# An MLP kernel in three stages: all up products, results kept in DRAM, then all down products as seven block products

## The chip, the cores and the metric

The kernel runs on one core of one Trainium2 chip. The metric is device time of one execution in microseconds (us), the median of several runs. TensorE is called PE, VectorE DVE, ScalarE ACT, GpSimd POOL; SP is the engine whose queue issues most loads.

## The reference

Four batches of 448 tokens. Attention with 12 heads of 64 and capped scores gives x (448 x 768 per batch); a low-rank product over the tokens (U, V, rank 32) is added to it; then comes a two-layer MLP of width 3,072 with a residual.

```python
def _attn_ref(q, k, v, cap):
    scores = scale * np.matmul(q, k.transpose(0, 1, 3, 2))
    scores = cap * np.tanh(scores / cap)
    ...
    attn = np.exp(scores)
    attn = attn / (np.sum(attn, axis=-1, keepdims=True) + 1e-09)
    return np.matmul(attn, v).astype(np.float32)

def _moe_ref(x, U, V, w_ch1, w_ch2):
    xt = x.transpose(0, 2, 1)
    h = xt @ U @ V
    u = x + h.transpose(0, 2, 1)
    ch = np.maximum(u @ w_ch1, 0.0) @ w_ch2
    return (u + ch).astype(np.float32)
```

All is float32. On PE a float32 product of the MLP is made of three matmuls on fp32r operands: each operand is split into a high and a low part (ACT copies the high part, DVE subtracts to get the low one), and high x high, high x low and low x high are added in PSUM.

## The kernel before

The program is written as a list of tasks, each with the engines that it can run on, an estimated duration, the buffers that it reads and writes, and a priority. A planner (`Plan.simulate`, lines 133 to 228) walks through time with these estimates, hands out buffers of the pools as they come free, and so fixes the order of instructions on every engine; `emit` then writes them in that order. Nothing is reordered on the chip: each engine executes its own list, and waits where an operand or a buffer is not ready.

The token activations after attention are u0 to u3, one for each batch, with the 768 features on partitions (six blocks of 128) and the 448 tokens in a row.

*Up products* (`up_seven`, matmuls on line 867). The batches go in two pairs, (0, 1) and (2, 3). The 24 blocks of 128 hidden features go in 12 chunks of two. For a pair and a chunk, the two halves of the 768 features, the two blocks and the two batches make a 2 x 2 by 2 x 2 block product, done by Strassen's scheme in seven products of nine matmuls (three feature blocks times the three parts), 63 matmuls of 128 x 128 by 448 for each chunk. Its operands are sums and differences: x for the activations (seven tiles for a pair, built once for each pair by `operands` and `part`, lines 695 and 702) and ws for the weights (built for each chunk from wa, `strassen_weights`). Results go from PSUM through cx, are added up (line 880), and pass a relu. The up products make 1,512 matmuls.

*Weights.* Both matrices arrive as 64-bit words; `convert` (lines 309, 314, 317) turns a raw block wr of 768 KB into 384 KB of float32 wa, which ACT's queue also stores to DRAM (kept, line 728) so that the second pair of batches loads it from there (line 718).

*Down products.* For the first pair (`down`, line 948) each chunk is followed by 12 plain products of six matmuls, interleaved with the up products of the next chunk by their priorities. For the second pair, the first ten chunks are joined in twos (QUADS = 5) and the down product of four hidden blocks is done in seven products (`down_seven`, line 1075; operands in `down_operands`, lines 994 and 1001), 126 matmuls for each; the last two chunks take the plain way. Together 1,008 plain matmuls and 630 in seven products. The results are added into u, either by DVE from PSUM (lines 953, 1093) or by a copy to st on ACT and an accumulating DMA on POOL's queue (lines 961, 1098), which the code calls a pour.

*Attention* (`four`, `normalize`, `mixin`) stands ahead of all this on PE and overlaps only a little with the first chunk. The sums over keys for the softmax are matmuls with a block of ones (line 585); for heads from number ALONE = 12 on, the part of the keys that is left over (64 of 448) has four small matmuls of its own for each pair of heads (line 588, in the profile each counted twice), while for the first 12 heads DVE adds it beforehand (line 552, 64 x 896).

## Time and profile before

| | |
|---|---|
| median of 3 runs | 842.54 us (842.36 to 843.48) |
| the profiled execution | 842.78 us, its span 841.0 us |
| PE busy | 832.0 us (99%) |
| DVE, ACT, POOL busy | 675.6, 498.2, 123.5 us |
| HBM read, written | 79.28 MB, 24.47 MB |

The profile is one execution. Busy times are from the first to the last of overlapping instructions; matmuls are pipelined, so their single durations (0.366 us) are longer than the distance between two of them. What ended an engine's idle time is inferred from semaphores.

### The profile page before, as it was taken

The page shows a single profiled execution, that of the slowest core. Times are in us where ns is not written, and L with a number is a line of the kernel's source. Part 1 is how long each engine was busy: PE and PEld are TensorE (multiplying, and loading weights), DVE is VectorE, ACT ScalarE, POOL GpSimd, SP SyncE. Part 2 cuts the span into 40 slices and gives each one's busy share as a digit, 9 for nine tenths or more (in the row PEclk, how much of TensorE's full clock was granted, in tenths as well). Part 3 has the DMA queues.
Part 4 walks back from the last instruction along what each step waited for, and adds up shares of the span by engine and source line. Part 5 has one row for each costly group of instructions (what it writes and reads, how often), then busy time and mean ns, then how long its engine had stood idle before and what let it go on. Part 6 is the DMA issues. An engine that isn't in the chain of part 4 may idle for free.

```text
span 841.0 us, 12164 instructions
## 1 busy us (share of the span) xinstructions
PE 832.0 (99%) x4524; PEld 663.2 (79%) x4524; DVE 675.6 (80%) x1141; ACT 498.2 (59%) x748; POOL 123.5 (15%) x162
## 2 busy tenths in 40 slices
PE   9999999999999999999999999999999999999998
PEld 4343333337899999999999999999999999999997
DVE  4778999659878878887888899698797887978764
ACT  7989999876545544454455445365565555555510
POOL 0111111111111111111111112001121111211200
PEclk9999999999999999999999999999999999999999
DMA  6456554513878867867686747526346263642413
GB/s 228 132 158 208 152 179 121 168 46 117 254 217 220 262 198 216 237 189 214 205 266 160 207 102 192 148 60 157 71 97 152 44 157 78 134 108 44 103 32 131
DMA packets 47612, 129.64 MB, mean 154 GB/s; under 512 B 6178, under 2 KB 23618, under 8 KB 47554
## 3 DMA queue, kind: packets, MB, share of 16 engines
q1 hardware_dynamic: 23024, 79.29, 29.7%
q0 software_dynamic: 17616, 30.71, 20.1%
q10 hardware_dynamic: 6914, 18.88, 5.7%
q8 instruction: 35, 0.57, 0.3%
q14 instruction: 23, 0.19, 0.1%
HBM read 79.28 MB, written 24.47 MB: 123 GB/s over the span
## 4 chain that ended last, share of the span: by engine, by line
PE 95%; DVE 2%; DMA 1%; ACT 1%; issue 1%; POOL 0%; DVEq 0%; POOLq 0%; ACTq 0%
PE mm L867 36%; PE mm L948 24%; PE mm L1075 15%; PE sc L488 8%; PE o L546 6%; PE misc L662 1%; PE o L531 1%; PE misc L585 1%; PE misc L405 1%; DMA rd<-r 1%; PE misc L651 1%; PE misc L635 1%; DVE x L702 1%; DMA rb<-rd 0%; PE misc L588 0%
## 5 line engine op out<-in xcount | busy, mean ns | idle before, releaser
L867 PE MATMUL mm<-x,ws 128*128 128x448 f32 x1512 | 330.7, 366 | 0.8 <-ACT cx L263 0.8
L867 PEld LDWEIGHTS mm<-x,ws 128*128 128x128 f32 x1512 | 283.3, 188 | 27.5 <-ACT cx L263 1.8
L948 PE MATMUL mm<-g,w 128*128 128x448 f32 x864 | 187.0, 366 | 0.0
L948 PEld LDWEIGHTS mm<-g,w 128*128 128x128 f32 x864 | 162.1, 188 | 13.8 <-issue 0.2
L1075 PE MATMUL mm<-g,w 128*128 128x448 f32 x630 | 139.2, 366 | 0.0
L1075 PEld LDWEIGHTS mm<-g,w 128*128 128x128 f32 x630 | 118.3, 188 | 9.7
L263 ACT ACTIVATE st<-mm 128x448 f32<-128x448 f32 x109 | 59.2, 543 | 80.7 <-PE mm L948 48.7
L961 POOL DMA_DIRECT2D u<-st x60 | 51.7, 862 | 272.3 <-ACT st L263 272.3
L953 DVE TENSOR_TENSOR u<-u,mm 128x448 f32<-128x448 f32 x108 | 66.1, 618 | 29.3 <-PE mm L948 28.9
L488 PE MATMUL sc<-qk 64*128 64x448 f32 (+1 forms) x384 | 77.4, 571 | 0.4 <-ACT th L495 0.4
L506 ACT ACTIVATE th<-th,capt 128x1792 f32<-128x1792 f32 x42 | 75.3, 1792 | 0.8
L495 ACT ACTIVATE th<-sc 128x896 f32<-128x896 f32 x80 | 69.6, 915 | 5.1 <-PE sc L488 4.9
L1098 POOL DMA_DIRECT2D u<-st x45 | 38.9, 864 | 211.6 <-ACT st L263 174.1
L488 PEld LDWEIGHTS sc<-qk 64*128 64x128 f32 (+1 forms) x384 | 27.6, 175 | 41.3 <-issue 18.1
L546 PE MATMUL o<-th,vn 128*64 128x448 f32 x280 | 57.9, 548 | 0.0
L263 ACT ACTIVATE cx<-mm 128x448 f32<-128x448 f32 x42 | 22.9, 546 | 57.4 <-PE mm L867 49.3
L702 DVE TENSOR_TENSOR ws<-ta,ws 128x384 fp32r<-128x384 f32 x96 | 52.8, 554 | 3.1 <-ACT ws L263 2.2
L263 ACT ACTIVATE ws<-ta 128x384 fp32r<-128x384 f32 x57 | 29.5, 520 | 34.6 <-PE mm L867 22.6
L317 DVE SCALAR_TENSOR_TENSOR wa<-wa,wr 128x768 int32<-128x768 int32 (+2 forms) x50 | 46.6, 932 | 4.0 <-ACT wa L309 3.3
L263 ACT ACTIVATE ws<-wa 128x384 fp32r<-128x384 f32 x51 | 26.0, 520 | 39.5 <-PE mm L867 39.5
L552 DVE TENSOR_TENSOR es<-es,th 128x896 f32<-128x896 f32 (+1 forms) x36 | 39.1, 1086 | 11.6 <-ACT th L506 10.9
L309 ACT ACTIVATE wa<-wr 128x768 f32<-128x768 f32 (+2 forms) x50 | 44.3, 888 | 6.9 <-DVE cx L880 1.9
(123 smaller groups left out, 932.3 us busy)
## 6 DMA issues: line engine op xcount, KB each, us to landing
wr<-in_w SPq DMA_DIRECT2D x48, 768.0 KB, 6.7
u<-st POOLq DMA_DIRECT2D x105, 224.0 KB, 4.2
kept<-wa ACTq DMA_DIRECT2D x48, 384.0 KB, 6.4
wa<-kept SPq DMA_DIRECT2D x28, 384.0 KB, 3.7
qk<-in_qk SPq DMA_DIRECT2D x23, 448.0 KB, 4.1
wr<-kept SPq DMA_DIRECT2D x20, 384.0 KB, 4.0
vn<-in_v SPq DMA_DIRECT2D x12, 448.0 KB, 3.9
rb<-rd POOLq DMA_DIRECT2D x24, 224.0 KB, 3.8
```

The costliest lines, as they stand in the source:

```text
L263: e.activation(out=out, in_=in_, func=func)
L317: nc.vector.scalar_tensor_tensor(out=a_t().bitcast(I32), in0=a_t().bitcast(I32), scalar=3, in1=raw_t()[:, 0::2], op0=ALU.logical_shift_lef ...
L488: nc.tensor.matmul(ps.t[out, a, :S], qks[c].t[hd, 1, 128 * t:min(S, 128 * t + 128)], qks[c].t[hd, 0], start=True, stop=True)
L495: nc.scalar.activation(out=th.t[:, j], in_=ps.t[:, :, :S], func=AF.Tanh, scale=(self.half if t == 3 else self.qsc) if raw else 1.0)
L506: nc.scalar.activation(out=th.t, in_=th.t, func=AF.Exp, scale=self.capt)
L546: nc.tensor.matmul(o.t[64 * a:64 * a + 64, :S], vn.t[:, 3 * i + t, a], th.t[:, j, a], start=False, stop=t == 2)
L702: e.tensor_tensor(out=lo, in0=src(), in1=hi.bitcast(F32), op=ALU.subtract)
L867: nc.tensor.matmul(ps.t[:, :S], ws[p].t[:, wi, sl], xs[p].t[:, xi, d], start=fresh and n == 0, stop=n == 8, skip_group_check=not fresh)
L948: nc.tensor.matmul(ps.t[:, :S], w1[f].t[:, wi, sl], g[b, f].t[:, gi], start=f == fs[0] and i == 0, stop=f == fs[-1] and i == 2)
L953: nc.vector.tensor_tensor(out=u.t[:, d], in0=u.t[:, d], in1=ps.t[:, :S], op=ALU.add)
L961: nc.gpsimd.dma_start(out=u.t[:, d], in_=st.t, accum_op=ALU.add)
L1075: nc.tensor.matmul(ps.t[:, :S], w[:, wi, k, sl], g[gi][:, k], start=fresh and n == 0, stop=n == 5, skip_group_check=not fresh)
```

## The change

The MLP runs in three stages. First come the up products of the pair (0, 1), then those of the pair (2, 3), both for all 12 chunks with no down products in between (`moe`, `up_seven`). Each result, 448 values on 128 partitions, is stored to DRAM (mid) by POOL's queue as soon as its relu is done. Then `down_all` makes all down products: the 24 hidden blocks form six quads m, two quads form a group, and for each group and each of the seven products the weights are built and split once and used for both pairs of batches (n); for each pair three output blocks of 12 matmuls are made. Two quads add up in one PSUM bank. That is 3 x 7 x 2 x 3 x 12 = 1,512 matmuls. `down`, `down_operands`, `down_seven`, `last_sums` and `weights` are removed.

The second weight matrix is converted block by block when there is room (SECONDS: 4 blocks in the first stage, 12 in the second, 8 in the first group of the third) and stored in DRAM by quads; stage 3 loads its weights (wb) and tokens (gq, gw) from DRAM. Every third result is poured (EVERY = 3), except in the last two products. For all heads DVE now adds the left-over keys (RESTS = 24). The pools are cut anew: attention has four more th tiles, stage 3 takes over memory of closed pools. The planner has a model of the transfer time of DMAs (size).

```diff
-QUADS = 5
-PORDER = 2, 3, 1, 6, 5, 7, 4
+GROUPS = (0, 1), (2, 3), (4, 5)
+EVERY = 3
+SECONDS = (0, 0, 1, 0, 1, 0, 1, 0, 1, 0, 0, 0), (0, 0, 1, 1, 1, 1, 1, 2, 1, 2, 1, 1), (2, 2, 2, 2)
+PORDER = 2, 1, 3, 6, 5, 7, 4
...
-FILL, FIRST = 14, 3
+RESTS = 24
+FILL, FIRST = 11, 3
...
+            done = now + cost + OVER.get(e, 0) + (LAT[e] if t.lat is None else t.lat)
+            if t.size:
+                self.moved = max(self.moved, now + cost + 1800) + t.size
+                done = max(done, self.moved + 500)
+            heapq.heappush(events, (done, 2, t.i, "d"))
...
-        self.wp = Pool("wp", {"wa": 2, "w1": 3, "g": 3, "ws": 4, "ta": 3}, shared={"gp": "g"})
+        self.wp = Pool("wp", {"wa": 2, "ws": 4, "ta": 3})
-        self.pre = Pool("pre", {"th": 3, "qk": 2, "es": 2})
-        self.xe = Pool("xe", {"x": 3, "cx": 2}, after=(self.pre,), shared={"st": "cx"})
+        self.pre = Pool("pre", {"th": 7, "qk": 2, "es": 2})
+        self.wg = Pool("wg", {"wl": 2, "wb": 2, "g": 3}, after=(self.pre,), shared={"wa": "wb"})
+        self.xe = Pool("xe", {"x": 3, "cx": 2}, after=(self.pre,), under=(self.wg,))
...
+        self.wc = Pool("wc", {"wb": 4}, after=(self.late,), within=(self.wp, "ws"))
+        self.wt = Pool("wt", {"wt": 2}, after=(self.late,), within=(self.wp, "wa"))
+        self.cl = Pool("cl", {"gq": 9, "st": 2}, after=(self.xe,))
+        self.cr = Pool("cr", {"wb": 4, "wt": 2, "wl": 1, "wr": 1, "wa": 1, "gq": 2, "g": 4}, after=(self.late,), side="right")
...
-                if p < ALONE:
+                if p < RESTS:
...
+            if which:
+                m, k, j = f // 4, f // 2 % 2, f % 2
+                if (m, j) not in self.quads:
+                    self.quads[m, j] = self.dp.tile([128, 2, DM], F32, tag="quad", name="quad", bufs=NF // 2)
+                nc.scalar.dma_start(out=self.quads[m, j][:, k], in_=a.t)
+                return
...
+            ws = None if n else self.strassen_weights(0, True, 60000, ALONE - 90)
...
+                prio = 3 if n or c < NCH - 2 else -60
+                ws = ws or self.strassen_weights(c, n == 0, 0, prio)
+                for _ in range(SECONDS[n][c]):
+                    self.block(1, next(seconds), True, 0, 3)
+                self.up_seven(n, c, xs, ws, order)
+                ws = None
+                order += 21
+        self.down_all(order, seconds)
...
+        if not begin:
+            at = iter([order - 4, *at][:1] + list(range(order + 3, order + 21, 3)))
...
+        def result(b, j, x):
+            self.task({"ACT": 560}, lambda: self.copy(nc.scalar, to(x), to(x), AF.Relu), r=[key(x)], w=[key(x)], prio=-200)
+            store(b, j, x)
+        def store(b, j, x):
+            at = n, c // 2, b, j
+            def out():
+                if at not in self.mid:
+                    self.mid[at] = self.dp.tile([128, 2, S], F32, tag="mid", name="mid", bufs=2 * NF)
+                nc.gpsimd.dma_start(out=self.mid[at][:, c % 2], in_=to(x))
+            self.task({"POOL": 1000}, out, r=[key(x)], w=[("mid", at, c % 2)], lat=4000, size=620, prio=-200)
...
+    def down_all(self, order, seconds):
...
+        for ms in GROUPS:
+            a, b, s2, w, g, bank = {}, {}, {}, {}, {}, {}
+            last = ms is GROUPS[-1]
+            for x, p in enumerate(PORDER):
+                for _ in range(SECONDS[2][x - 3] if ms is GROUPS[0] and x > 2 else 0):
+                    self.block(1, next(seconds), True, 0, prio, (self.cr,))
+                for m in ms:
+                    for i, j in {2: ((0, 1),), 1: ((0, 0),), 3: ((1, 0), (1, 1))}.get(p, ()):
...
+                for n in range(2):
+                    for m in ms:
+                        at = {2: (1, 0), 3: (1, 1), 1: (0, 0), 6: (0, 1), 7: (1, 0)}.get(p)
+                        if at:
+                            b[(m, n, *at)] = token(m, n, *at)
...
+                        if p == 6:
+                            term(b01, b11, ALU.subtract, b01, size)
+                            term(b00, b01, ALU.add, b00, size)
+                        if p == 5:
+                            term(b11, b11, ALU.subtract, b00, size)
+                        if p == 7:
+                            term(b10, b10, ALU.subtract, b00, size)
+                        src = {3: b11, 1: b00, 6: b00, 5: b11, 2: b10, 7: b01, 4: b10}[p]
+                        hi, lo = g[p, n, m] = [self.buf("g", [128, 2, S], F32R, self.wg, *self.gx, self.cr) for _ in range(2)]
+                        split(src, (hi, lambda hi=hi: hi.t), (lo, lambda lo=lo: lo.t), size)
+                for n, bs in enumerate(((0, 1), (2, 3))):
+                    u0, u1 = (self.u_bufs[i] for i in bs)
+                    for d in range(3):
+                        fresh = p not in (6, 5, 4)
+                        if fresh:
+                            bank[p == 3, n, d] = self.bank()
+                        ps = bank[p == 3, n, d]
+                        def products(p=p, n=n, d=d, ps=ps, fresh=fresh, w=w, g=g, ms=ms):
+                            sl = slice(128 * d, 128 * d + 128)
+                            at = [(m, k, wi, gi) for m in ms for k in range(2) for wi, gi in ((0, 0), (0, 1), (1, 0))]
+                            for i, (m, k, wi, gi) in enumerate(at):
+                                nc.tensor.matmul(
+                                    ps.t[:, :S], w[p, m].t[:, wi, k, sl], g[p, n, m][gi].t[:, k], start=fresh and i == 0,
+                                    stop=i == len(at) - 1, skip_group_check=not fresh)
+                        self.task({"PE": 6 * 206 * len(ms)}, products, r=[
...
+                        onto = {3: ((u1, d),), 1: ((u0, d),), 6: ((u0, 3 + d),), 5: ((u1, d), (u1, 3 + d)), 2: ((u0, d),),
+                            7: ((u1, 3 + d),), 4: ((u0, 3 + d),)}[p]
+                        for u, e in onto:
+                            count += 1
+                            self.onto(ps, lambda u=u, k=e: u.t[:, k], (u, e), count % EVERY == 0 and not (last and p in (7, 4)))
+                            if last and p in (1, 5, 7, 4) and (p != 5 or e < 3):
+                                self.task({"SP": 350}, lambda u=u, k=e, i=bs[u is u1]: nc.sync.dma_start(
+                                    out=self.out[i, 128 * k:128 * k + 128], in_=u.t[:, k]), r=[(u, e)], lat=2500, size=700, prio=-200)
```

On PE, in the steady part of the first pair, before (mm is the PSUM bank, x and ws the up operands, g the relu'd tokens, w1 the second weights):

```order
L948 MATMUL mm_2285<-g_2090,w1_1992 128x448 x3
L948 MATMUL mm_2285<-g_2139,w1_2222 128x448 x3
L948 MATMUL mm_2297<-g_2090,w1_1992 128x448 x3
L948 MATMUL mm_2297<-g_2139,w1_2222 128x448 x3
L867 MATMUL mm_2306<-x_1125,ws_2150 128x448 x9
L948 MATMUL mm_2323<-g_2090,w1_1992 128x448 x3
L948 MATMUL mm_2323<-g_2139,w1_2222 128x448 x3
L948 MATMUL mm_2333<-g_2090,w1_1992 128x448 x3
L948 MATMUL mm_2333<-g_2139,w1_2222 128x448 x3
L867 MATMUL mm_2272<-x_1056,ws_2176 128x448 x9
```

and on PE in the changed kernel, its whole list from the last steps of attention (misc) to the end:

```order
L812 MATMUL mm<-x,ws 128x448 x9
L672 MATMUL misc<-vst,ys 128x448 x2
L812 MATMUL mm<-x,ws 128x448 x27
L645 MATMUL misc<-ident,u_1401 112x64 x16
L812 MATMUL mm<-x,ws 128x448 x9
L661 MATMUL misc<-xx,ust 32x128 x8
L812 MATMUL mm<-x,ws 128x448 x9
L672 MATMUL misc<-vst,ys 128x448 x2
L812 MATMUL mm<-x,ws 128x448 x1413
L958 MATMUL mm<-g,wl 128x448 x12
L812 MATMUL mm<-x,ws 128x448 x9
L958 MATMUL mm<-g,wl 128x448 x1500
```

Up and down products no longer alternate; one set of 12 down matmuls stands ahead of the last nine up matmuls.

On DVE, where the x operands of the second pair are built (u_1002, u_1451 are u2 and u3; wr holds the differences), before:

```order
L265 CAST x<-wr 128x448 x2
L702 TENSOR_TENSOR x<-wr,x 128x448 x3
L953 TENSOR_TENSOR u_562<-u_562,mm 128x448
L695 TENSOR_TENSOR wr<-u_1002,wr 128x448 x3
L880 TENSOR_TENSOR cx<-cx,mm 128x448
L702 TENSOR_TENSOR x<-wr,x 128x448 x2
L835 SCALAR_TENSOR_TENSOR g<-cx,g 128x448
L953 TENSOR_TENSOR u_562<-u_562,mm 128x448
L702 TENSOR_TENSOR x<-wr,x 128x448
L695 TENSOR_TENSOR wr<-u_1002,u_1451 128x448
```

and in the changed kernel (u_974, u_1401 are u2 and u3):

```order
L274 CAST x<-wr 128x448 x2
L712 TENSOR_TENSOR x<-wr,x 128x448 x3
L705 TENSOR_TENSOR wr<-u_974,wr 128x448
L825 TENSOR_TENSOR cx<-cx,mm 128x448
L705 TENSOR_TENSOR wr<-u_974,wr 128x448
L712 TENSOR_TENSOR x<-wr,x 128x448
L705 TENSOR_TENSOR wr<-u_974,wr 128x448
L712 TENSOR_TENSOR x<-wr,x 128x448
L825 TENSOR_TENSOR cx<-cx,mm 128x448
L712 TENSOR_TENSOR x<-wr,x 128x448
L705 TENSOR_TENSOR wr<-u_974,u_1401 128x448 x3
L712 TENSOR_TENSOR x<-wr,x 128x448 x3
```

The adds of down products (line 953) and the low parts of g (line 835) are gone from between, and the operands of different products follow each other directly.

On SP's queue, before, in the part of the second pair with seven products (wa and wr are loads of kept weights):

```order
L718 DMA wa<-kept 128x768 x5
L982 DMA wr<-kept 128x768 x2
L718 DMA wa<-kept 128x768
L982 DMA wr<-kept 128x768 x2
L718 DMA wa<-kept 128x768 x4
L982 DMA wr<-kept 128x768 x4
```

and in the changed kernel from the first loads of stage 3 on (wb weights, gq and gw tokens, wr raw blocks of the second matrix):

```order
L884 DMA wb<-quad 128x2x384 x2
L891 DMA gq<-mid 128x896 x2
L891 DMA gw<-mid 128x896
L884 DMA wb<-quad 128x2x384 x4
L891 DMA gw<-mid 128x896
L734 DMA wr<-in_w 128x1536
L884 DMA wb<-quad 128x2x384 x2
L891 DMA gq<-mid 128x896 x9
L884 DMA wb<-quad 128x2x384 x2
L734 DMA wr<-in_w 128x1536 x2
```

Tokens, which stayed in SBUF before, are now loads on this queue, 448 KB each, beside the weights.

## Rows read from the trace of the kernel before

**Rows 1.** The page: busy times, granted clock in tenths, chain by engine.

```profile
PE 832.0 (99%) x4524; PEld 663.2 (79%) x4524; DVE 675.6 (80%) x1141; ACT 498.2 (59%) x748; POOL 123.5 (15%) x162
...
PEclk9999999999999999999999999999999999999999
...
PE 95%; DVE 2%; DMA 1%; ACT 1%; issue 1%; POOL 0%; DVEq 0%; POOLq 0%; ACTq 0%
```

**Rows 2.** PE's waits, first and last: us in total, times, longest.

```profile
PE o L531 <- ACT th L506: 1.6, 2, 0.9
...
PE sc L488 <- ACT th L495: 0.4, 1, 0.4
```

**Rows 3.** Stretches: length; busy us by engine; clock, DMA share, GB/s.

```profile
60.00:150.00 90.00, 87.35 (x658) 32.31 (x660) 83.72 (x133) 85.94 (x94) 14.50 (x24) 1.00 0.58 175
150.00:188.00 38.00, 38.00 (x285) 13.49 (x277) 22.05 (x32) 30.63 (x32) 6.33 (x11) 1.00 0.31 93
188.00:841.00 653.00, 648.26 (x3240) 593.51 (x3238) 532.78 (x916) 329.26 (x572) 96.39 (x113) 1.00 0.57 154
```

**Rows 4.** Chain that ended last, its pieces: start us, us, what.

```profile
511.77 14.57 PE mm L948 x72
526.34 27.43 PE mm L867 x135
...
807.93 29.11 PE mm L948 x144
```

**Rows 5.** Timeline of PE in attention: start us, us, what.

```profile
161.36 0.94 PE L588 MATMUL misc<-th,ones 128*32 128x448 f32 x8
162.22 1.77 PE L488 MATMUL sc<-qk 64*128 64x448 f32 x8
```

**Rows 6.** Groups by line: form, count, busy us, mean ns; DVE's left-over keys.

```profile
L552 DVE TENSOR_TENSOR es<-es,th 64x896 f32<-64x896 f32 x12 | 13.0, 1083 | 0.3
```

**Rows 7.** Timeline of DVE, back to back.

```profile
516.96 0.35 DVE L265 CAST ws<-wa 128x384 fp32r<-128x384 f32 x1
517.23 0.55 DVE L702 TENSOR_TENSOR ws<-ta,ws 128x384 fp32r<-128x384 f32 x1
517.70 0.55 DVE L702 TENSOR_TENSOR ws<-wa,ws 128x384 fp32r<-128x384 f32 x1
...
519.64 0.95 DVE L1001 TENSOR_TENSOR w<-wr,w 128x768 fp32r<-128x768 f32 x1
520.51 0.61 DVE L953 TENSOR_TENSOR u<-u,mm 128x448 f32<-128x448 f32 x1
521.04 0.55 DVE L702 TENSOR_TENSOR ws<-ta,ws 128x384 fp32r<-128x384 f32 x1
```

**Rows 8.** DMA queues, 225 to 450 us: packets, MB, share; one landing.

```profile
q1 hardware_dynamic: 4859, 26.51, 38.0%
q0 software_dynamic: 5904, 9.41, 24.1%
q10 hardware_dynamic: 4896, 13.37, 15.0%
...
u<-st POOLq DMA_DIRECT2D x41, 224.0 KB, 4.8
```

**Rows 9.** Table of stretches where the second pair's x operands are built.

```profile
485.00:500.00 15.00, 15.00 (x76) 13.91 (x75) 14.65 (x30) 7.08 (x15) 1.72 (x2) 1.00 0.44 97
500.00:512.00 12.00, 12.00 (x60) 11.07 (x59) 11.85 (x22) 6.43 (x13) 2.60 (x3) 1.00 0.24 40
512.00:526.34 14.34, 14.34 (x72) 13.31 (x72) 12.33 (x24) 6.33 (x13) 3.43 (x4) 1.00 1.01 282
```

**Rows 10.** Tile st: POOL's issues, ns min/median/max; landing us.

```profile
L961 POOL DMA_DIRECT2D u<-st x60: 842/864/931, 215.2 to 527.5; - x60
...
DMA to landing us min/median/max: 3.1/4.0/8.9
```

336 lines of the change are left out of this document (73 added, 263 removed).

## Prediction

> **What bounds the kernel now.** I read the page's busy table first. TensorE (PE) is busy 832.0 of 841.0 us at the full granted clock in every slice, and 95% of the chain that ended last is PE [rows 1]. A busy PE alone proves little, so the second view is the list of PE's waits. It has five, together 5.1 us; its first and its last row stand in [rows 2]. From 188 us to the end the stretch table has PE busy 648.3 of 653 us, with the last add and store in the rest [rows 3]. There the time is the number of matmuls times their spacing. The pieces of the chain give it: 144 in 29.11 us are 0.2022 us each, 135 up matmuls in a row in 27.43 us are 0.2032 [rows 4]. So a matmul that is removed there is time, until another engine is late.
>
> Who would be late next? From 60 to 150 us, in the attention, ACT is busy 85.9 and VectorE (DVE) 83.7 of 90 us, both near PE's 87.4; from 150 to 188 us ACT has 30.6 and DVE 22.1 of 38 [rows 3]. Behind 188 us DVE is the nearest, 533 of 653.
>
> **The change part by part.** The profiled execution took 842.78 us against a median of 842.54; its span is 841.0, so 1.8 us lie around the span. I sum against the span and add 1.5 at the end (1.8 less the 0.2 by which this execution lies over the median).
>
> *Matmuls.* In the order of before stand 3,150 block matmuls behind the attention: 1,512 up, 1,008 plain down, 630 in seven products. Now both halves are seven products and there are 1,512 + 1,512 = 3,024. The difference is 126 x 0.2022 = **-25.5 us**, all on the path.
>
> *The sums of attention (RESTS 24).* Six groups of four small matmuls on line 588 go. One stands from 161.36 to 162.22 us, where the next begins [rows 5]: 0.86 each, 5.2 us. Three of the six lie before 150 us, where ACT is nearly as full as PE and might give nothing back: between -2.6 and -5.2. In their place DVE gets twelve adds of 1.08 us [rows 6], half of them before 150 us, where it had 6.3 us free. That can cost 0 to 2 us. I take **-4.5** for both. The three filler matmuls that go stood in PE's idle time at the start: nothing.
>
> *Slots on DVE.* One instruction begins before the last has ended. In [rows 7] 0.35 us takes a slot of 0.27, 0.55 takes 0.47, 0.95 takes 0.87, 0.61 takes 0.53: the slot is the mean less 0.08. With these I count what the new order lets DVE do between two block matmuls, numbered from 1 in PE's order.
>
> *Stage 1, up to matmul 631.* The loads are those of before in 127.4 us of matmuls (and 5.4 of leftover attention) where before had more than twice as long. In this stretch SP issues 18.9 MB, ACT 9.0 MB and GpSimd (POOL) 37 stores of 0.229 MB. From 225 to 450 us SP's queue q1 moved 26.51 MB with 38.0% of the engines, 0.310 MB/us at full share; ACT's q10 0.396; POOL's q0, all accumulating, 0.174 [rows 8]. A plain POOL store is not in the trace in this form. Its bounds are ACT's stores (same direction) and POOL's accumulating ones: 21 or 49 us. With 60.9 for SP, 22.8 for ACT and 2 for the last broadcast that is 107 to 135 us of 132.8. So 0 to 2 us; I take **+0.5**, since ACT's stores are the nearer kind.
>
> *Join of the two batch pairs.* Before, 72 down matmuls in one piece, 14.57 us [rows 4], stood where the x operands of the second pair are built. Now up products stand there alone. Between matmul 757 and 946 (38.2 us of PE) DVE has 23 instructions with a slot of 0.54, 36 of 0.47, 8 of 0.28, 3 of 0.48, 5 of 0.87 to 1.01 and two short casts: 38.2 us, all of it. Before, DVE did 26.5 us of work in the 27 us from 485 to 512 and PE waited for nothing [rows 9], so a full DVE need not cost. But x slots come free one product at a time: a product lasts 9 x 0.2022 = 1.8 us and an x operand with a difference costs DVE 6 x 0.54 = 3.2. Three of them follow each other (6, 3, 7), so up to 3 x 1.4 = 4 us. I take **+2** (0 to 4), between the quiet stretch and this lag.
>
> *Start of stage 3.* Now every operand of the down products comes back from DRAM. Between matmul 1,513 and 1,702 (38.2 us of PE) SP issues 10 weight tiles, 13 token tiles and 2 raw blocks, 11.5 MB or 37.0 us at 0.310; ACT one store, 1.0; POOL five accumulating pours, 6.6, and the last plain store, 1. That is 45.6 us of transfer, 7.4 too many. Between 1,828 and 1,954 (25.5 us) it is 7.8 MB from SP, two stores, six pours: 25.2 + 2.0 + 7.9 = 35.1, again 9.6 too many. What hides it is the lead: g has nine buffers, and a set of one product for both pairs takes eight, so DVE and the loads run about one set (72 matmuls, 14.6 us) ahead. Bounds: 0, if the lead covers both, and 17, if it covers nothing. I take **+4**, nearer to 0, because in the 14.3 us from 512 us the DMA engines were full (share 1.01) and PE was busy throughout [rows 9].
>
> On this the Trainium skill speaks too: DMA: Bandwidth & Descriptors, Specifications, gives about 358 GB/s as a core's share of HBM. By that the first stretch's 13.2 MB would take 37 us of 38.2 and the second's 10.0 MB 28 of 25.5, and this term would be about 0.5 (an estimate from that page), the time 816.5. The row decides: SP's queue moved 0.310 MB/us of full share [rows 8].
>
> *DVE in stage 3.* Between 1,702 and 2,080 (76.4 us) it has 25 slots of 0.54, 37 of 1.01, 25 of 0.87, 6 of 0.48: 75.3 us, 98%, nearly three times as long as the full stretch of before [rows 9]. Its instructions stand in order, and one add that waits for PE holds the splits behind it. 0 to 4, I take **+1**. ACT is at half there. The end of the program keeps its form: a product, an add, a store.
>
> Sum: 841.0 - 25.5 - 4.5 + 0.5 + 2 + 4 + 1 = 818.5 of span, 820.0 us.
>
> **The rivals.** *Nothing waits.* Before, PE stayed busy with DVE and DMA full for a while [rows 9]. If that holds here, all added terms are nothing: 841.0 - 25.5 - 4.5 + 1.5 = 812.5, or 811.8 with all 5.2. Against it: these stretches are longer now, and two of them hold more transfer than time.
>
> *DMA bounds stage 3.* The two excesses count whole and stage 1 and the join take their upper ends: 841.0 - 25.5 - 4.5 + 2 + 4 + 17 + 1 + 1.5 = 836.5; with the excesses whole and the other terms as I took them 833. For it: pours and loads share the engines, and loads are queued in order on SP. Against: the lead of one set.
>
> *Slower: the result buffers.* In stages 1 and 2 an up result leaves its buffer cx only when its store has landed; before, a relu freed it. There are five buffers, so 5 x 12.7 = 63.7 us of buffer time in a chunk of 63 matmuls. Without the landing the four results need 13.0 + 3.9 + 3.9 + 1.4 = 22.2 (c22 waits six products, c11 and c12 one; add, relu and POOL's issue are 0.62 + 0.58 + 0.86). Four landings fit up to (63.7 - 22.2)/4 = 10.4 us each. From there a microsecond more costs 4/5 us in each of 24 chunks, 19 us. With landings of 12.0 it is 31 us on top of 820: 851, slower. The pours landed after 4.8 us (median) beside the heaviest loads [rows 8] and after 8.9 at most [rows 10], so it needs more than twice the median.
>
> The Trainium skill has a rule that would push this way: SBUF — State Buffer, "SBUF: two separate sides", says that VectorE in a mode that uses both ports locks GpSimd out, and that a DMA issued from GpSimd then waits for its descriptors, some 2.5 us in its example. By it landings would be 7.3 us (an estimate from that page), still under 10.4, but nearer, and I would give this rival 0.08 instead of 0.04. The trace does not bear it out: POOL's issues took 842 to 931 ns, median 864, beside all kinds of DVE work [rows 10].
>
> **How the numbers follow.** Forecast with small waits, 814 to 829 us: 0.65. Nothing waits, 811 to 814: 0.12. DMA bounds stage 3, 829 to 838: 0.17. Slower, above 844: 0.04. Within 0.2% of 842.5 (what a measurement of this kernel can tell from no change): 0.02, as the far end of DMA. The range is 812.5 to 832: it leaves out half of the upper case and the slower one. Faster 0.94, same 0.02, slower 0.04.
>
> **What would show it.** The matmuls: 3,024 with the same spacing, 0.202. The attention: the first up matmul at 183 to 184 us instead of 187.9. The join and stage 3: PE's list of waits names cx, x or ws around 350 us and g or wl between 510 and 620 us, and PE is busy without a gap behind matmul 2,080. The transfer: a DMA share near 1 in the two stretches. I am wrong if waits are spread evenly over stages 1 and 2 (result buffers), if DVE is idle while PE waits in stage 3 with the loads landed, or if the spacing of matmuls has changed.

## The result, and the profile after

The changed kernel takes 831.55 us (median of 4 runs, 830.93 to 833.18), the kernel before in the same comparison 842.45. The ratio is 0.9873 with a 95% interval of 0.9855 to 0.9892: 10.9 us faster, where 22.5 were forecast. The profiled execution took 831.91 us, its span is 830.1.

The page of after: busy times, granted clock, chain by engine.

```profile
PE 806.4 (97%) x4344; PEld 637.7 (77%) x4344; DVE 678.1 (82%) x1068; ACT 481.1 (58%) x685; POOL 120.6 (15%) x193
...
PEclk9999999999899999999999999999999999999999
...
PE 67%; issue 11%; DVE 9%; DMA 7%; ACT 3%; POOL 2%; SPq 0%; POOLq 0%; DVEq 0%; ACTq 0%
```

Against [rows 1]: PE is no longer 95% of the chain but 67%; DVE, DMA and ACT have come in. One slice, at 207 to 228 us, has a lower clock. PE's list of waits shows where the chain leaves PE (us in total, times, longest); [rows 2] had five, together 5.1 us:

```profile
PE mm L812 <- ACT cx L272: 8.7, 7, 4.0
PE o L541 <- ACT th L516: 3.7, 4, 1.1
PE misc L645 <- DVE u L624: 2.1, 2, 1.2
PE misc L672 <- DVE ys L274: 1.8, 2, 1.1
...
PE mm L958 <- DVE g L903: 0.6, 1, 0.6
```

The costliest is an up product that waits for the copy `cx<-mm`, by which ACT takes a bank's sum out before the next product adds onto it. Only 0.8 us of waits lie in stage 3. The table of stretches of after (columns as in [rows 3]):

```profile
60.00:150.00 90.00, 86.23 (x630) 31.44 (x626) 80.65 (x124) 85.55 (x94) 13.80 (x23) 1.00 0.46 142
150.00:188.00 38.00, 34.46 (x254) 12.38 (x251) 30.31 (x43) 30.56 (x33) 6.05 (x11) 1.00 0.39 116
188.00:222.00 34.00, 27.92 (x171) 20.91 (x170) 27.18 (x52) 17.75 (x35) 4.91 (x9) 0.90 0.58 182
222.00:515.47 293.47, 289.18 (x1413) 264.27 (x1413) 244.90 (x479) 162.97 (x295) 49.15 (x90) 1.00 0.71 240
```

and before in the third of these stretches:

```profile
188.00:222.00 34.00, 33.23 (x217) 25.92 (x216) 29.79 (x55) 19.24 (x37) 4.15 (x6) 1.00 0.50 153
```

In 188 to 222 us, where up products begin and attention ends, PE does 171 matmuls where it did 217: 27.9 us of work for 33.2, and at a mean granted clock of 0.90. That is the largest single loss.

From PE's timelines the sum can be made again, matmul against matmul. Before, the first up matmul stands at 187.94 us and PE ends at 837.03; after, at 187.67 and 826.45, and stage 3 begins with block matmul 1,504 at 515.47.

| term | forecast | measured |
|---|---|---|
| 126 matmuls less | -25.5 | -25.6 |
| attention, to the first up matmul | -4.5 | -0.3 |
| stages 1 and 2, to 515.47 us | +2.5 | +13.3 |
| stage 3 | +5 | +2.0 |
| behind PE's end | 0 | -0.3 |
| sum | -22.5 | -10.9 |

The first row is what block matmuls 1,504 to 1,629 took before. The third is how much later matmul 1,504 begins, counted from the first: 327.8 us for 314.5. The fourth is what the last 1,521 took: 311.0 for 309.0. Of the 13.3 us, 7.4 are lost by matmul 127 (229 us), which begins 41.5 us behind the first one where it was 34.0; 5.9 come behind it, one wait of 1.55 where the pairs join among these.

**How the 7.4 us come about.** Pieces of the chain that ended last, after, 184 to 216 us:

```profile
187.85 6.65 DMA rb<-rd
...
194.59 1.09 DVE u L624
195.68 0.47 DVE ws L712
...
198.90 2.13 DVE x L712 x4
...
205.65 1.62 issue
207.27 0.04 ACT wa L323
207.31 0.78 issue
208.09 0.53 ACT cx L272
208.62 0.04 issue
208.67 6.43 PE mm L812 x18
```

The broadcast rb of the softmax sums lands after 6.65 us. DVE's next instruction, the normalizing add of line 624, needs it and stands idle 2.77 us; the splits of x stand behind it, and behind these the sums of weights `ta<-wa` (line 705). On ACT the convert of line 323 stands ahead of the copy `cx<-mm` that PE needs. The chain calls the 1.62 us before the convert "issue"; ACT's sequencer and DVE show what it waited for. First ACT's row for line 323 (ns min/median/max of its semaphore waits, first and last start), then DVE:

```profile
L323 ACTq EVENT_SEMAPHORE  x2: 17/1164/2310, 204.9 to 204.9; - x2
```

```profile
206.64 0.55 DVE L705 TENSOR_TENSOR ta<-wa,ta 128x384 f32<-128x384 f32 x1
```

The convert waits 2.31 us, from 204.9 to 207.2, and DVE's `ta<-wa` ends at 207.19: the buffer wa that the convert fills was still being read. The raw block that it converts is late as well, since the differences of x lie in a raw buffer (`wr`) that comes free late, so that SP issues the load at 199.99 us; but it took 4.3 us to land and was there at 204.3, before ACT came to it:

```profile
DMA to landing us min/median/max: 4.3/4.3/4.3
```

PE's timeline:

```profile
202.61 2.08 PE L812 MATMUL mm<-x,ws 128*128 128x448 f32 x9
208.67 6.43 PE L812 MATMUL mm<-x,ws 128*128 128x448 f32 x18 [3.97 <-ACT cx L272]
```

PE waits 3.97 us, and the 18 matmuls behind the wait take 6.43 us; at 190.59 us 18 of them take 3.91. Before, DVE did not wait for the broadcast at this place, and SP's first load there stood at 197.34 us; after, a load of a raw block and a store of a converted one are issued at 186.38, a microsecond ahead of the broadcast. The traces say that these slow it: in before, e1, e2 and e16, where neither is on its way, the two broadcasts of this place land after 3.3 to 3.6 us; in every other kernel those that were issued behind the two take 5.8 to 7.7. Landings of the two in before and in after:

```profile
DMA to landing us min/median/max: 3.3/3.4/3.4
```

```profile
DMA to landing us min/median/max: 6.5/6.6/6.6
```

Moving the load alone was not tried.

### The profile page after: what moved, and what is told of

The parts are those of the page before. It is cut to its first block, busy times and chain, and to the rows that moved or that the text cites. A ratio compares the mean times of both kernels' runs of the same rounds, so it can differ in the third digit from the quotient of the medians.

```text
span 830.1 us, 11899 instructions
## 1 busy us (share of the span) xinstructions
PE 806.4 (97%) x4344; PEld 637.7 (77%) x4344; DVE 678.1 (82%) x1068; ACT 481.1 (58%) x685; POOL 120.6 (15%) x193
## 4 chain that ended last, share of the span: by engine, by line
PE 67%; issue 11%; DVE 9%; DMA 7%; ACT 3%; POOL 2%; SPq 0%; POOLq 0%; DVEq 0%; ACTq 0%
PE mm L958 33%; PE mm L812 23%; PE sc L498 4%; PE o L556 3%; DVE es L562 2%; POOL mid L838 2%; DMA quad<-wa 2%; DMA rb<-rd 1%; DMA wb<-quad 1%; DVE x L712 1%; ACT th L505 1%; DMA rd<-r 1%; DVE g L903 1%; ACT th L516 1%; DMA mid<-cx 1%
## 5 line engine op out<-in xcount | busy, mean ns | idle before, releaser
L958 PE MATMUL mm<-g,wl 128*128 128x448 f32 x1512 | 308.5, 366 | 0.8 <-DVE g L903 0.6
L958 PEld LDWEIGHTS mm<-g,wl 128*128 128x128 f32 x1512 | 283.7, 188 | 25.3 <-DVE g L903 1.2
L272 ACT ACTIVATE st<-mm 128x448 f32<-128x448 f32 x44 | 24.0, 544 | 120.5 <-issue 85.6
L838 POOL DMA_DIRECT2D mid<-cx x96 | 52.9, 551 | 263.5 <-ACT cx L272 253.5
L272 ACT ACTIVATE cx<-mm 128x448 f32<-128x448 f32 x96 | 49.0, 543 | 57.4 <-PE mm L812 41.2
L903 DVE TENSOR_TENSOR g<-gq,g 128x896 fp32r<-128x896 f32 x62 | 67.1, 1086 | 12.5 <-ACT g L272 11.6
L983 POOL DMA_DIRECT2D u<-st x44 | 38.2, 876 | 238.8 <-ACT st L272 211.6
L272 ACT ACTIVATE g<-gq 128x896 fp32r<-128x896 f32 x62 | 57.8, 944 | 22.5 <-PE mm L958 9.8
L825 DVE TENSOR_TENSOR cx<-cx,mm 128x448 f32<-128x448 f32 x72 | 44.3, 615 | 19.6 <-PE mm L812 16.3
L272 ACT ACTIVATE cx<-cx 128x448 f32<-128x448 f32 x72 | 41.7, 579 | 31.1 <-DVE cx L825 30.1
```

Of the source, the lines that this page charges most:

```text
L272: e.activation(out=out, in_=in_, func=func)
L838: nc.gpsimd.dma_start(out=self.mid[at][:, c % 2], in_=to(x))
L903: self.task({"DVE": 130 + 1.09 * size}, lambda: nc.vector.tensor_tensor(out=lo(), in0=src.t, in1=hi().bitcast(F32), op=ALU.subtract), r=[( ...
L958: nc.tensor.matmul(ps.t[:, :S], w[p, m].t[:, wi, k, sl], g[p, n, m][gi].t[:, k], start=fresh and i == 0, stop=i == len(at) - 1, skip_group ...
```

## Experiments

All times beside the runs of the kernel before on the same chip (842.3 to 842.6 us). The planner deals all rows anew with each edit, except in e5, e8 and e13. A trace is of one execution of the range: the fastest in e3, e4, e9 and e15, the slowest in e5, e7, e14 and e16.

| kernel | median (range), us | ratio to before, 95% |
|---|---|---|
| after | 831.55 (830.93 to 833.18) | 0.9873, 0.9855 to 0.9892 |
| e1_rests12 | 832.94 (827.99 to 835.91) | 0.9878, 0.9854 to 0.9903 |
| e2_before_rests24 | 845.07 (843.16 to 846.41) | 1.0031, 1.0020 to 1.0042 |
| e3_bcast_late | 828.95 (825.41 to 829.73) | 0.9832, 0.9816 to 0.9849 |
| e4_own_bank | 836.84 (834.53 to 838.35) | 0.9932, 0.9920 to 0.9945 |
| e5_start_36more | 837.27 (835.91 to 841.46) | 0.9950, 0.9931 to 0.9969 |
| e6_every2 | 833.74 (831.91 to 838.66) | 0.9905, 0.9884 to 0.9925 |
| e7_interleaved | 834.98 (834.57 to 837.28) | 0.9912, 0.9899 to 0.9925 |
| e8_stage3_36more | 838.69 (838.30 to 841.27) | 0.9966, 0.9953 to 0.9980 |
| e9_store_on_act | 827.81 (826.75 to 829.84) | 0.9829, 0.9816 to 0.9842 |
| e10_no_double | 829.59 (828.09 to 829.96) | 0.9844, 0.9831 to 0.9857 |
| e11_stage1_free | 839.04 (835.29 to 839.92) | 0.9947, 0.9929 to 0.9964 |
| e12_four_buffers | 835.40 (832.90 to 838.36) | 0.9914, 0.9897 to 0.9930 |
| e13_fill_wait | 833.30 (830.88 to 835.92) | 0.9897, 0.9879 to 0.9915 |
| e14_adds_on_pool | 832.38 (831.04 to 833.69) | 0.9882, 0.9869 to 0.9896 |
| e15_both_cures | 828.71 (827.02 to 832.03) | 0.9848, 0.9829 to 0.9867 |
| e16_qk_late | 832.78 (830.56 to 837.86) | 0.9886, 0.9867 to 0.9904 |

### The attention: e1, e2, e14

**e1**

```diff
-RESTS = 24
+RESTS = 12
```

> The changed kernel with the left-over keys of the last 12 heads summed by PE again (RESTS 12), nothing else edited. Before and after, the first up matmul stands at 187.94 and 187.67 us, so the attention gave 0.3 us and not the 4.5 of the prediction. Theory A (PE's six groups of 0.86 us went, but the twelve adds made DVE the last in attention, so that PE's time came back as waits): putting the groups back costs nothing, 831.5 within 1.0, first up matmul at 187 to 188 us, and PE's waits between 60 and 188 us fall from 7.3 us to 2 to 4. Rival (the saving is in the time, and something else that the change did to the attention, the pools and the wider lead, ate it): 835 to 837, first up matmul at 191 to 193 us.

**e2**, in the kernel before:

```diff
-                if p < ALONE:
+                if p < 24:
...
-        rest = p >= ALONE
+        rest = p >= 24
```

> The kernel before with this one part of the change alone: the left-over keys of all 24 heads are summed by DVE. Theory A (no room on DVE, whatever the rest of the program): 842.5 within 1.0, first up matmul at 187 to 188.5 us, new PE waits in place of the six groups. Rival (room is there, and other parts of the change took it): 838 to 839, first up matmul at 183 to 184 us.

e2 is the clean one: this part alone makes the kernel before 2.7 us slower, where theory A had it the same within 1.0. The first up matmul comes at 189.19 us, not 187.94. PE's row that waits for ACT's exponentials, in e2 and then in e1 ([rows 2] have 1.6 for before):

```profile
PE o L531 <- ACT th L506: 3.7, 4, 1.1
```

```profile
PE o L541 <- ACT th L516: 1.5, 2, 0.9
```

With PE's sums (before, e1) 1.6 and 1.5 us, with DVE's adds (e2, after) 3.7 and 3.7: some 2.2 of the 5.2 us that PE saves it then waits for ACT, whatever the rest of the program. In e2 all waits of 60 to 188 us together grow from 2.65 to 7.53 us (those of 0.3 us and more): those for ACT from 1.6 to 5.2, those for DVE from 1.1 to 2.4. That PE's time comes back as waits is theory A; that DVE would be the last is not, ACT has the larger part.

e1 does not fit it so simply. Without the adds the attention ends 5.9 us later (first up matmul at 193.59), as the rival says, and yet the time is that of after within the interval. PE's waits between 60 and 188 us did not fall as theory A has it: 7.6 us, for 7.3. The start of stage 1 loses less instead: waits of 2.4 us from 189 to 225 where after has 6.1. And 3.4 of e1's waits in the attention come from a load of q and k on which DVE stood 3.92 us. So a microsecond of the attention is not a microsecond of the kernel. To separate ACT from DVE, the adds went to POOL.

**e14**

```diff
-                    self.task({"DVE": 1090}, partial(add, in0=some, ...
+                    self.task({"DVE": 1090} if p < ALONE else {"POOL": 2500}, partial(add, in0=some, ...
```

> The changed kernel with the twelve left-over adds of the last 12 heads on POOL, which is busy for 15% of the time, and neither on DVE nor on PE. It tells apart what took the gain of the attention: with the sums on PE (before, e1) PE waits 1.5 us for ACT's exponentials, with the adds on DVE (after, e2) 3.7 us, and the other 3 us of waits between 60 and 188 us are for DVE. If DVE's row took the rest (ys, u, xx, r late), these waits fall by 2 us and the first up matmul comes at 185 to 186 us, time 829 to 831; the 3.7 us for ACT stay. Rival (ACT alone holds the end of attention, DVE's waits are its shadow): first up matmul at 187.5 within 0.7, 831.5 within 1. An add of POOL could also take so long that the sums come late: then 834 and more.

Stretches of e14:

```profile
150.00:188.00 38.00, 37.06 (x270) 15.36 (x267) 31.09 (x43) 31.28 (x34) 19.05 (x17) 1.00 0.46 129
188.00:250.00 62.00, 55.52 (x303) 46.37 (x302) 51.06 (x97) 35.20 (x65) 9.77 (x17) 0.92 0.70 227
```

In this trace the attention part came out as the theory has it: PE's waits in 60 to 188 us fall from 7.3 to 4.5, the first up matmul comes at 184.77, and 3.3 us for ACT stay. By it DVE's row held some 3 us. e15, which has the adds on POOL too (planned at 2.3 us, not 2.5), does not repeat it: waits of 8.8 us and the first up matmul at 189.62, where e9 without them has 187.91. So what DVE's row holds is not shown. And the time did not follow (832.4): from 188 to 250 us PE does no more than in after and the clock is lower. The start of stage 1 takes the 3 us back.

### The start of stage 1: e3, e5, e8, e13

**e3**

```diff
-            lat=7800 if p == 1 else 5000 if p < 20 else 3800
+            lat=7800 if p == 1 else 5000 if p < 20 else 7000
```

> The changed kernel, with the planner told that the broadcast of the reciprocal sums for the last heads lands 7.0 us after its issue and not 3.8 (6.65 were measured in the chain). Only the order changes: the normalizing add on DVE (line 624) stands behind six or so splits of x and not ahead of them. Theory B (the add that waits 2.77 us at the head of DVE's row makes the x splits late, so the raw block of weights is loaded late, so its convert stands on ACT ahead of the copy cx<-mm for which PE waits 3.97 us, and the clock falls for the next 18 matmuls): the wait of 3.97 us and the slow 18 matmuls (6.43 us where 3.67 is the rule) go together, 824 to 827. If only the wait shrinks and the clock still falls: 828. Rival (three PSUM banks at that place are too few, or the load of the second chunk's weights is late by itself): the wait stays where it is, 831.5 within 1.0.

DVE of e3, and its stretch:

```profile
194.26 1.16 DVE L712 TENSOR_TENSOR x<-wr,x 128x448 fp32r<-128x448 f32 x2
195.33 1.09 DVE L624 TENSOR_TENSOR u<-u,rb 128x896 f32<-128x896 f32 x1
```

```profile
188.00:222.00 34.00, 30.75 (x196) 23.36 (x195) 31.43 (x59) 20.31 (x40) 5.70 (x11) 1.00 0.65 215
```

The add now stands behind five splits and waits for nothing. The wait of 3.97 us is gone (the longest there is 1.04), the clock is 1.00, PE does 196 matmuls for 171. Matmul 127 begins 36.3 us behind the first, for 41.5 in after and 34.0 before. The profiled execution, the fastest of four, is 6.5 us shorter than after's, as theory B says; the median gains 2.6 (828.95, where theory B gave 824 to 827), and the other three runs lie at 828.8 to 829.7. Where they lose it no trace shows.

The place of theory B holds. In all kernels with this edit but e16 (41.1 us) matmul 127 begins 34.0 to 37.2 us behind the first; in those without it, e5 and e13 with their added matmuls left aside, 40.0 to 42.7, except in e1 (37.3), whose broadcast took 3.4. One link of the theory is wrong: not the load but the buffer wa, still read by DVE, held the convert. And e3 moves more than the add: on ACT the planner put the copy ahead of the convert, so e3 does not tell the two apart.

```profile
202.86 0.53 ACT L272 ACTIVATE cx<-mm 128x448 f32<-128x448 f32 x1
203.29 0.90 ACT L323 ACTIVATE wa<-wr 128x768 f32<-128x768 f32 x1
```

**e5** (36 matmuls at the start) and **e8** (36 in stage 3), all other engines' rows as in after:

```diff
+                for turn in range(5 if begin and p == 2 else 1):
```

```diff
+                        def products(..., turns=2 if last and p == 2 and n == 0 else 1):
...
+                            for i, (m, k, wi, gi) in [*enumerate(at)] * turns:
```

> The changed kernel with 36 matmuls more on PE at the start of stage 1: product 2 of the first chunk is made five times over (each time from zero, the last counts). The planner does not know of them, so the order on all other engines is that of the changed kernel. 36 x 0.204 = 7.3 us. Theory D (at the start the time is set by the chain that brings the second chunk's weights, and not by PE: before, a chunk's 63 up matmuls were followed by 72 plain down matmuls that need no new up weights, 27 us for a chunk, now the second chunk is wanted 12.8 us after the first began): the wait of 3.97 us and the slow matmuls behind it are filled, and the 36 cost 0 to 2 us: 831.5 to 833.5. Rival (PE's list sets the time there too, the wait moves on by as much): 837.5 to 839.

> The changed kernel with 36 matmuls more in stage 3 (product 2 of the last group is made twice for the first pair, each time from zero): the counterpart of e5 at another place. If PE's matmuls set the time of stage 3, they cost 36 x 0.204 = 7.3 us: 838 to 839.5. Rival (DVE with 98% of the time, or the transfers, set it, and PE is carried along): 832 to 835.

e8 costs 7.1 us of 7.3: in stage 3 a matmul is time, and the term of the sum stands. e5 costs 5.7, nearer to its rival: for the time as a whole theory D, that the start has a fixed time of its own, falls. At the place itself it is right in part: the wait of 3.97 us became one of 2.31 at 214.28 us, the clock stayed at 1.00, and by matmul 127, the added ones left out, e5 is 2.6 us later than after for 7.3 us of work put in. In this trace, the slowest of six, the rest came later, among it a wait of 2.56 us at 293.49 for a copy behind a late store.

**e13**

```diff
+                for turn in range(3 if n0 == 0 and c == 1 and p == 5 else 1):
```

> The changed kernel with 18 matmuls more on PE just ahead of the wait of 3.97 us at 208.67 us: product 5 of the second chunk is made three times over (each time from zero, the last counts). The planner does not know of them; all other engines keep their order. 18 x 0.204 = 3.7 us, as long as the wait. If the slow 18 matmuls behind that wait (6.43 us where 3.67 is the rule, granted clock 0.94 from 188 to 250 us) are the price of PE's idleness by itself, then the wait is filled, the clock stays at 1.00, and the kernel gets faster by the 2.8 us of the slow stretch in spite of the added work: 828 to 829.5. Rival (the clock falls for another reason, the wait moves on by the length of what was added): 833 to 835.5.

```profile
203.31 5.74 PE L813 MATMUL mm<-x,ws 128*128 128x448 f32 x27
210.93 5.48 PE L813 MATMUL mm<-x,ws 128*128 128x448 f32 x18 [1.89 <-ACT cx L272]
```

The 3.7 us that were put into the wait made it 2.1 us shorter; it moved on, and behind what is left of it (1.89 us) 18 matmuls still took 5.48. By matmul 127, the added ones left out, e13 is 0.4 us later than after, so in this trace the start hid 3.3 of the 3.7. The median rises by 1.75, and the intervals of e13 and after overlap. My theory expected a faster kernel; it failed, since the wait could not be filled. On PE the lower clock costs 2.5 us in after (6.43 for 3.91) and 1.6 in e13; what the kernel would gain without it stays open.

### The rest of stages 1 and 2: e4, e7, e9, e10, e11, e12

**e4**

```diff
-            fresh = onto not in bank
+            fresh = onto not in bank or p == 6 and n + c > 1
...
```

> The changed kernel, where from the third chunk on product 6 of an up chunk opens a bank of its own and does not add onto product 1's. That leaves product 1 out of three of the four results; all instructions, loads and stores stay, the one thing that goes is that product 6 waits for the copy cx<-mm of product 1. Theory C (PE's waits behind 222 us, 0.58, 0.58, 1.55, 0.21 and 1.30 us, all for a copy cx<-mm, come from this: between the copy and the next matmuls onto the bank stands one product, 1.8 us, where before plain down products stood as well): most of them go, 827 to 829. Rival (the copies are late since x, ws or cx are late, and PE would wait for those next): the waits come back under other names, 831.5 within 1.0.

```profile
367.33 5.86 PE L812 MATMUL mm<-x,ws 128*128 128x448 f32 x20 [4.22 <-DVE ws L712]
```

5 us slower than after, and so outside both expectations. Where PE no longer waits for the copy, it runs into the next shortage, here the weights ws at the join, in one long wait of 4.22 us with slow matmuls behind it. Theory C falls.

**e7**

```diff
+        if 1 < c < NCH - 1:
+            at = iter(range(order, order + 42, 6))
```

> The changed kernel with the broadcast's landing put right as in e3, and the products of neighbouring chunks in turn on PE from the third chunk to the eleventh of either pair: one of this chunk, one of the next. So between the copy of a bank and the next product that adds onto it stand two or three products and not one. Everything is computed. Theory C in its second form (own_bank removed one of three such dependences, and PE met the next; here all of them get more cover): e3's waits between 225 and 500 us, 0.38, 1.55, 0.31 and 1.47 us, shrink to the one at 360 us, where the pairs join: 826 to 827.5. Rival E (in stages 1 and 2 PE is as fast as its weights, a chunk's worth every 12.9 us, and where a wait for a copy goes, one for ws comes, longer and with a fall of the clock behind it, as in own_bank): 829 to 835.

6 us slower than e3 (its edit is in e7 too): waits of 9.1 us between 225 and 500 us where e3 has 3.7, now named by DVE's adds `cx` too (five, 3.2 us). That two chunks in turn hold twice the banks and results is the likely cause, and not shown. Another 4.4 us of waits lie in stage 3, where e3 has 0.4, most of them for DVE's g. More cover for a copy does not help; the second form of theory C falls as well.

**e9**, **e10**, **e11**, all on e3, and **e12** on after:

```diff
-                nc.gpsimd.dma_start(out=self.mid[at][:, c % 2], in_=to(x))
+                nc.scalar.dma_start(out=self.mid[at][:, c % 2], in_=to(x))
...
-            self.task({"POOL": 1000}, out, ...
+            self.task({"ACT": 120}, out, ...
```

> Kernel e3 with the 96 stores of up results on ACT's queue, behind the relu on the same engine, and not on POOL's. In e3 ACT waited 4.8 us (6 times, 225 to 500 us) for such a store to land before it could copy the next bank out; the landings took 2.2 to 8.0 us. Theory (the result buffers matter in small: not the mean landing of 4.2 us but the late ones make ACT wait, and PE behind it): with POOL's issue of 0.55 us and one change of engines less in the life of a buffer the waits for mid<-cx halve, 826.5 to 828.5 against e3's 829.0. Rival (the landing is set by the traffic, whatever the queue, and ACT's row now holds 96 issues more): 829 to 831.

```diff
-SECONDS = ..., (0, 0, 1, 1, 1, 1, 1, 2, 1, 2, 1, 1), (2, 2, 2, 2)
+SECONDS = ..., (0, 0, 1, 1, 1, 1, 1, 1, 1, 1, 2, 2), (2, 2, 2, 2)
```

> Kernel e3 with the 12 blocks of the second matrix that fall in stage 2 dealt one to a chunk up to the tenth, and two in each of the last two chunks; before, the eighth and the tenth chunk had two. The wait of 1.0 to 2.4 us that every kernel of this study has at 441 to 460 us follows a late load wa<-kept, whose buffer was held by the store of a block of the second matrix. Theory: it goes, 827 to 828. Rival (the wait comes from the loads' own time and appears elsewhere): 829 within 0.7.

```diff
-SECONDS = (0, 0, 1, 0, 1, 0, 1, 0, 1, 0, 0, 0), (0, 0, 1, 1, 1, 1, 1, 2, 1, 2, 1, 1), (2, 2, 2, 2)
+SECONDS = (0, 0, 0, 0, 0, 0, 0, 0, 0, 0, 0, 0), (0, 0, 1, 1, 1, 1, 2, 2, 2, 2, 2, 2), (2, 2, 2, 2)
```

> Kernel e3 with no blocks of the second matrix in stage 1: all 16 that stage 1 and 2 had are in stage 2, two to a chunk from the seventh on. In stage 1 a chunk takes 13.2 us on average (233.9 to 366.1 us, ten chunks) where 63 matmuls take 12.85. Theory (the four blocks, 4.7 MB of transfer and 6 us of ACT and DVE each way, make stage 1 short): stage 1 gains 2 to 3 us and stage 2, with 12.9 us for a chunk and DVE idle for a fifth of its time, loses 1: 827 to 828. Rival (every block costs what it costs, stage 2 loses as much in waits as at 455 us): 829 to 832.

```diff
-            for w in ((self.aq, "ust"), (self.aq, "vst"), (self.an, "sr"))]
+            for w in ((self.aq, "ust"), (self.aq, "vst"))]
```

> The changed kernel with four result buffers cx and not five (one of the three that take attention's memory is left out). By the arithmetic of the prediction, four buffers are 4 x 12.8 = 51.2 us of buffer time in a chunk; the four results need 22.2 without their landings, which leaves (51.2 - 22.2)/4 = 7.2 us for a landing, and the median is 4.2. By that means nothing changes: 831.5 within 1. Rival (late landings, up to 8.0 us, count one by one, and PE waits for each): PE's and ACT's waits for cx and mid<-cx between 225 and 500 us double from 4 and 4.5 us, 835 to 841.

e9 is the fastest kernel of the study, 827.8 us, but its interval meets e3's, and ACT's waits for stores did not halve (6.0 us for 4.8): its theory is not borne out. e10 changes nothing: at 448.93 us a wait of 1.2 us remains under another name (DVE's add `cx`), and one of 1.3 comes at 476. e11 misses both expectations: 10 us slower than e3. ACT's waits in e11, 225 to 500 us:

```profile
ACT cx L272 <- DMA mid<-cx: 11.2, 9, 2.8
ACT wa L323 <- DMA quad<-wa: 9.4, 4, 3.2
```

A converted block holds its buffer wa until its store has landed, and with two blocks to a chunk ACT stands before the next convert, with PE's copies behind it (PE waits 11.0 us there). So in stage 2 room for such blocks is short, and four of them are cheaper in stage 1. e12 costs 3.9 us, but not by the waits I named: ACT's waits for stores fell to 1.1 us, as I read it since the planner knew of four buffers and put other work first; PE lost it in one wait of 3.11 us at 458.71 (1.30 in after), the slow matmuls behind it, and one of 1.50 at 551.61 in stage 3. Neither expectation describes that.

### Stage 3: e6; and two combinations: e15, e16

```diff
-EVERY = 3
+EVERY = 2
```

> The changed kernel with every second down result poured (EVERY 2) and not every third: some 20 adds of 0.54 us leave DVE in stage 3, as many copies come to ACT and as many accumulating DMAs to POOL's queue. Theory (behind 500 us PE waited 0.8 us in all, both times for DVE; transfers had slack, though I charged 4 us for them): 830.5 to 832. Rival (the transfers were just under their limit, and more pours run into the loads): 834 to 840, with PE waiting for g or wl that wait for DMAs, between 510 and 620 us.

833.7, between the two: waits in stage 3 grow from 0.8 to 1.8 us, and the intervals of e6 and after meet. There was nothing to gain, and no cliff.

e15 is e9 with e14's adds on POOL; e16 is e9 with

```diff
-                    lat=3400 if p == 0 else 4200, prio=prios[i])
+                    lat=3400 if p == 0 else 5500, prio=prios[i])
```

> Kernel e9 (broadcast's landing put right, stores on ACT's queue) with the twelve left-over adds on POOL as in e14. In e14 alone the first up matmul came 3 us earlier, and the time stayed the same, because the second chunk's weights were late as before. If the two belong together (the earlier end of attention is worth something only where the start of stage 1 does not wait), it is 824 to 826 against e9's 827.8. Rival (the start has its own earliest time, whatever the attention does, or DVE, whose scalings and shifts got slower beside POOL's adds in e14, 0.65 us for 0.43 and 1.03 for 0.55, gives the 3 us back): 827 to 830.

> Kernel e9 with the planned landing of the loads of q and k at 5.5 us and not 4.2 (2.8 to 7.3 were measured in the kernel after, 4.0 the median; in e1 one of them made DVE wait 3.9 us and PE 3.4). Theory (what broadcasts did, other loads at the head of DVE's row do too): PE's waits for ys, u, xx between 60 and 188 us fall by 1 to 2 us: 826 to 827.5. Rival (the median was planned well, planning for the late ones holds buffers and gives nothing): 828 to 830.

e15 is its rival: 828.7, the two do not add. e16 misses: 5 us slower than e9, with a wait of 3.40 us at 221.07 and 2.29 at 170.81 in its slowest run. A planned landing nearer to the worst case is no cure in general; e3's was, for one instruction at one place.

## Why the prediction was wrong, step by step

The 831.55 us lie half a microsecond inside the range (812.5 to 832), and in the band that I gave to a stage 3 bound by DMA (829 to 838). That is luck: stage 3 lost 2.0 us, and the gain is 10.9 us and not 22.5 because two other terms failed, attention and stage 1.

**Matmuls, -25.5: right.** -25.6 by the profile, and e8 prices 36 of them at 7.1 us.

**Attention, -4.5: the step that failed first.** I took the 5.2 us of PE and allowed the adds 0 to 2 us, from DVE's spare time, over stretches. It measured -0.3. The profile before already had ACT at 85.9 of 90 us, and PE's saving came back as waits: against before, 3.6 us more for ACT and 1.3 more for DVE in e2, 2.6 and 2.1 in after. Alone the edit costs 2.7 us (e2). How much of it DVE's row alone holds stays open, since e14 and e15 differ. Busy time that is free over 90 us is not free where an instruction stands.

**Stage 1, +0.5: the term that was mis-sized most.** It was a balance of transfers over 133 us, and as a balance it was not wrong: in its fullest slices, 269.8 to 311.3 us, the DMA share was 0.92 and 0.93 and PE stood busy throughout. What it left out is the first chunk. There a broadcast, an add, splits, sums of weights, a convert and a copy follow each other, in rows that do not reorder, and by 229 us 7.4 us were lost against before. e3 shows the head of that chain.

**Join, +2: right in size, not in the way.** I had DVE late with the x operands. The wait of 1.55 us in after is for ACT: three copies of banks stand in a row there, the first of them waits for PE's own last product, and PE waits for the third, until 366.72 us:

```profile
365.25 1.42 ACT L272 ACTIVATE cx<-mm 128x448 f32<-128x448 f32 x3 [0.35 <-PE mm L812]
```

**Waits spread over stages 1 and 2.** I had written that this would prove me wrong, and put it down to result buffers. In after a copy is named in every one of them, but e4, e7, e9, e10 and e12 each took one cause away or eased it and the waits came back elsewhere. What they share, as I read it: behind 188 us before, PE had plain down products to turn to, which needed no new up weights; now one stage has one kind of work, and every late landing reaches PE. No run put down products back between the up products, so this is argued and not shown. The spread of the runs fits it: before's twelve runs beside e1 to e4 lie within 1.6 us, e1's six within 7.9.

**Stage 3, +5: too large.** It cost 2.0, of which 0.8 are waits. I sized the loads at 0.310 MB/us of full share [rows 8]. From 515 to 555 us q1 moved 10.85 MB with 73.2% of the engines, 0.371 MB/us, and from 580 to 607 us 0.392. The stretch:

```profile
580.00:607.00 27.00, 27.00 (x135) 24.85 (x134) 26.29 (x35) 12.77 (x18) 4.29 (x5) 1.00 1.06 355
```

The rate I took came from raw blocks and kept weights; the tokens and weights of stage 3 move faster. The Trainium skill, DMA: Bandwidth & Descriptors, Specifications, whose 358 GB/s would have made the term of its start 0.5, was nearer than my row: 355 GB/s stood here with PE busy throughout. The page calls its figure a limit; from 529 to 555 us 376 GB/s were measured here, and the measurement decides. And DVE at 98% cost 0.6 us for the 1 that I allowed: from 556 to 632 us it was busy 74.7 of 76 us.

**Slower by the result buffers: no.** Landings took 4.2 us at the median and 8.0 at most, under the 10.4 of the prediction.

**The sum.** The errors are +4.2 (attention), +10.8 (stages 1 and 2) and -3.0 (stage 3); with -0.4 from matmuls and the tail they make the 11.6 us between 818.5 and 830.1.

**What stays open:** how much of the loss is the lower clock by itself; what exactly the waits behind 229 us (5.9 us with the slow matmuls) come from, and whether they can be had back. Kernels with nearly the same work and other deals of it took 827.8 to 832.9 us (e9, e15, e3, e10, after, e14, e16, e1), so single causes under 2 us could not be told apart.

## What to carry to other kernels

When a change sorts two kinds of work that took turns into stages, price the first chunk of each stage as a chain of latencies (landing, add, split, buffer, convert, copy), not only as a balance of bytes and busy time; here it was 7.4 us by matmul 127. Work that leaves a full engine for one that is nearly full, beside a third that is nearly full, gives back little: try such a part alone in the kernel before (e2 here) ere it is counted. And an instruction that waits for a landing at the head of an in-order row is paid by all behind it: look there first. Planning for its late landing took 2.6 us off the median here (e3); doing the same for other loads (e16) did not help.
